# Two pairs of heads at the start of a hand-written order: scores ahead of w2's transposes, w2's fourth part ahead of v

## The chip, the cores and the metric

The kernel runs on one core of one Trainium2 chip. The metric is the device time of one execution in microseconds. The kernel before was run three times; the median counts. Beside these runs there is one execution taken by the hardware profiler, from which all durations come.

## The reference

Attention with a soft cap for 8 batches, 12 heads, 448 positions and head size 64, followed by a layer with two weights and a maximum:

```python
scores = cap * np.tanh(scale * (q @ k.T) / cap)          # cap 30
attn = np.exp(scores - max) / (sum + 1e-9)
x = (attn @ v)  -> (8 * 448, 12 * 64)
out = np.maximum(x @ w1, x @ w2) @ w_out                 # (768, 1024) twice, (1024, 768)
```

Inputs and output are float32. The kernel computes in bfloat16 with float32 sums. It doesn't subtract the row's maximum, since tanh bounds the scores. It writes the maximum as max(h1, h2) = h2 + relu(h1 - h2). So it needs x @ (w1 - w2), through a relu, times w_out, plus x @ (w2 @ w_out). The differences w1 - w2 (`wd_sb`) and the product w2 @ w_out (`wm_sb`) are made inside the kernel, in its first 60 us, beside the first pairs of heads.

## The kernel before, in words

The work is cut into **items** (two heads of one batch, 48 in all), **pairs** of items t (four heads, 24 in all) and, for the layer behind the attention, **groups** of matmuls (8 for each batch in stage 1, 6 or 8 in stage 2). No loop and no scheduler orders it. A string, `ORDER` (lines 9 to 202), lists steps by hand, and the last lines of the kernel (742 to 745) call them one after the other; each engine gets its instructions in that order, and waits for the other engines' results by semaphores. So the place of a step in the string is its place in the queue of each engine that it uses. The steps that matter here, with their lines:

- `ld0`, `cd` (L303, L308, L310): load k and q of items 0 and 1 as float32 over the SP and ACT queues, and cast them on ACT or DVE.
- `lk i`, `lq i` (L321 up to item 9, L328 after), `lv t part` (L352), `lw2 c` (L366), `lwo half part` (L360), `lw1 c` (L393): loads that cast on the way, all issued by POOL. Each of k and q is 112 KB as written, one part of w2 256 KB (512 KB as read), of w_out 384 KB, of v 128 KB. POOL has eight semaphores for its loads, so the ninth load waits until the first has landed, and so on.
- `dm`, `ms0`, `ms`, `id` (L734, L735, L289 to L292, L277): constants. `dm` sets the tile that the fillers read, `ms` the tiles of ones, `ms0` clears `ident` on DVE, and `id` writes its diagonal on POOL.
- `D bank n` (L471): idle matmuls of n units of 128 columns, four units in one instruction, whose result nobody reads. They keep PE busy where nothing else is ready.
- `X i bank` (`Xh` for half), `XC i` (L458, L463): transposes of k and q of an item on PE (28 small ones) into a PSUM bank, and DVE's copy out of it.
- `S i j`, `T i j` (L514, L519): scores of a block of 128 keys for both heads of an item (two matmuls), and their tanh on ACT. `L t`, `TL t` (L528, L532): the left-over 64 keys of a whole pair. `E i j0 j1`, `EL t` (L536, L539): the exponentials, in place.
- The scores have **two** PSUM buffers, given out in turn to S, L and VL. A step that takes a buffer waits until the tanh of its last user, or DVE's reading of the finished values, is done.
- `W c bank`, `WC c` (L416, L420): eight transposes of w2's part c on PE, and DVE's copy of them. `OP`, `P c half n`, `PC c half` (L431, L437): n matmuls of w2 @ w_out, eight for each c and half, and DVE's copy into `wm_sb`. `sub c` (L402): w1 - w2 on DVE.
- `Y t` (L566, L570, L573), `Y1` to `Y3` (L578 to L584): the sums of the exponentials, and their inverse on DVE. `VL t`, `V t u j0 j1` (L600, L606): the product with v. `N t u` (L618, L621): the division on DVE, which writes x.
- `A`, `B` (L548, L553): from pair 3 on, DVE adds the exponentials up ahead of `Y`.
- `O`, `M`, `ev`, `H`, `Hs` (L645, L640, L666, L700, L702): groups of the layer behind: open a PSUM bank, matmuls, relu or copy out. `st` (L676, L681) stores. `cr` (L475): transposes of k and q by DMA, from item 10 on.
- The other matmul results share four PSUM banks, `mm0` to `mm3`. The bank is the last number of `X`, `W`, `OP`, `Y` and `O` and the first of `D`. Who opens a bank waits until the bank's last result has been copied out.

In the first string PE gets W 2 (w2's third part) between the scores S 0 2 and S 1 0. A wait of a PE instruction holds up all that stands behind it in the string for PE.

Of the kernel before, what the change touches and what calls it, by code (L numbers as in the profile page):

```python
# [24 lines left out]
VL 2; V 2 0 0 3; V 2 1 0 3; S 7 0; OP 5 0 2; P 5 0 1; P 5 1 1; P 5 0 7; sub 0 0; Y1 2; Y2 2; Y3 2; N 2 0; N 2 1;  # L25
PC 5 1; A 3 0 1; PC 5 0; T 7 0; EL 3; lw1 1; lk 9 0; lq 10 0; lk 11 0; lw1 3; lq 9 0; lk 11 1; lv 3 1; lq 11 0;
lv 4 0; lv 3 0; lk 10 0; lw1 5; lk 10 1; O 0 0; M 0 -1 1; S 7 2; S 7 1; O 1 3; M 1 -1 1; M 0 -1 3; M 1 -1 1;
M 0 -1 2; T 7 1; T 7 2; Hs 0; S 8 0; M 1 -1 1; M 1 0 3; S 8 1; X 9 2; OP 4 1 1; P 4 1 4; sub 1 0; sub 3 0; XC 9;
E 7 0 2; T 8 1; T 8 0; P 4 1 4; L 4; O 2 2; M 2 0 2; S 8 2; M 2 0 1; M 2 1 3; A 3 0 2; A 3 1 1; B 3 1; PC 4 1;
ev 0; B 3 0; Hs 2; TL 4; E 7 2 3; T 8 2; S 9 0; O 3 1; M 3 1 3; M 3 2 3; O 4 0; M 4 2 3; VL 3; T 9 0; E 8 0 3;  # L30
A 3 1 2; ev 1; ev 2; sub 5 0; Hs 3; cr 5; V 3 0 0 1; Y 3 3; V 3 0 1 3; V 3 1 0 3; M 4 3 1; S 9 1; M 4 3 2; O 5 2;
M 5 3 3; lk 12 1; lk 13 0; lv 5 3; lq 13 0; lv 6 2; lv 4 1; lv 5 1; lk 12 0; lq 12 0; lk 15 0; lq 15 0; lk 13 1;
lq 14 0; lk 14 0; Hs 4; M 5 4 3; T 9 1; Y1 3; Y2 3; Y3 3; ev 3; N 3 1; N 3 0; Hs 5; O 6 3; M 6 4 3; M 6 5 3;
O 7 1; M 7 5 3; S 10 0; Hs 6; ev 5; A 4 0 1; ev 4; M 7 6 3; S 9 2; Hs 7; cr 6; EL 4; E 9 0 2; T 10 0; T 9 2;
O 8 2; M 8 6 2; S 10 2; M 8 6 1; M 8 7 3; S 10 1; O 9 0; M 9 7 2; T 10 2; T 10 1; E 9 2 3; M 9 7 1; VL 4;
V 4 1 0 2; L 5; TL 5; E 10 0 3; A 4 1 1; A 4 0 2; H 8; B 4 1; B 4 0; ev 7; A 4 1 2; ev 6; M 9 8 7; V 4 0 0 1;
Y 4 1; V 4 1 2 3; V 4 0 1 3; M 9 8 3; S 11 0; M 9 8 1; O 10 3; M 10 8 3; T 11 0; EL 5; Hs 9; Hs 8 2; Y1 4; Y2 4;
# [741 lines left out]
```

## Time and profile before

| what | us |
|---|---|
| three runs: median (lowest, highest) | 329.46 (329.17, 329.52) |
| the profiled execution: its own time | 329.59 |
| its span in the trace | 327.8 |
| PE busy (matmuls) | 320.3 |
| ACT busy | 281.2 |
| DVE busy | 240.2 |
| POOL busy | 161.7 |

The span runs from the first to the last instruction of the trace. Times in the trace count from its start. Matmul ends are modelled, so a PE that waits less than about 0.2 us can look busy; the step from one start to the next tells more than the length of one. The PE clock that the throttle granted was 1.0 throughout. Of DMAs the trace has the issue and the landing. In the groups and the timeline, a line stands for every step that comes through it.

### The profile page before, as it was taken

What the parts mean: (1) busy time and instruction counts of PE and PEld (TensorE: products, weight loads), DVE (VectorE), ACT (ScalarE), POOL (GpSimd) and SP (SyncE); (2) the same over time, 40 slices, a digit from 0 to 9 for tenths busy, and PEclk for the clock granted to TensorE, in tenths of its full rate; (3) what the DMA queues carried; (4) which work ended last, traced back from release to release, by engine and by line L of the source; (5) the groups of instructions that cost most, each with busy time, mean ns of one, the idle gap of its engine ahead of it and who ended that gap; (6) DMA issues with size and microseconds to landing.
All of it is one profiled execution on the core that took longest, in us unless ns stands there. A gap on an engine that the chain in (4) does not pass through costs nothing.

```text
span 327.8 us, 9768 instructions
## 1 busy us (share of the span) xinstructions
PE 320.3 (98%) x4137; PEld 184.6 (56%) x4140; DVE 240.2 (73%) x422; ACT 281.2 (86%) x278; POOL 161.7 (49%) x237
## 2 busy tenths in 40 slices
PE   8899999999999999999999999999999999999994
PEld 3445545446656664555565565556466556557662
DVE  3337889997887778987897688868878879873201
ACT  5899999999999999999999999999999999921120
POOL 8337387558862763754774675468538211000000
PEclk9999999999999999999999999999999999999999
DMA  8999999999999999999999999999999953013033
GB/s 186 193 201 134 289 185 168 115 127 137 202 187 102 118 193 194 123 79 170 165 184 90 212 138 184 109 177 142 188 114 90 211 154 46 2 50 98 0 98 96
DMA packets 134507, 46.28 MB, mean 141 GB/s; under 512 B 112320, under 2 KB 129472, under 8 KB 134464
## 3 DMA queue, kind: packets, MB, share of 16 engines
q0 software_dynamic: 94592, 25.02, 78.8%
q1 hardware_dynamic: 39424, 19.99, 28.2%
q8 instruction: 32, 0.52, 0.7%
q10 hardware_dynamic: 448, 0.66, 0.5%
q14 instruction: 11, 0.09, 0.1%
HBM read 47.78 MB, written 11.01 MB: 179 GB/s over the span
## 4 chain that ended last, share of the span: by engine, by line
PE 86%; DVE 6%; DMA 6%; POOL 1%; issue 1%; POOLq 0%; DVEq 0%
PE mm L645 58%; PE s L514 8%; PE s L606 8%; DMA w2b<-in_moe_w_dram 3%; PE mm L431 3%; DMA osb<-in_moe_w_dram 2%; PE s L528 2%; PE mm L573 1%; PE mm L640 1%; PE s L600 1%; DVE wd_sb L402 1%; PE mm L416 1%; DVE gT L666 1%; DVE xT L621 1%; POOL kqs L321 1%; PE mm L458 1%
## 5 line engine op out<-in xcount | busy, mean ns | idle before, releaser
L519 ACT ACTIVATE e<-s 128x896 bf16<-128x896 f32 x144 | 125.8, 928 | 6.3 <-PE s L514 6.0
L536 ACT ACTIVATE e<-e 128x1792 bf16<-128x1792 bf16 (+2 forms) x72 | 123.2, 1712 | 0.0
L645 PE MATMUL mm<-wo_sb,gT 64*128 64x384 bf16 x864 | 115.5, 323 | 0.0
L645 PE MATMUL mm<-wm_sb,xT 64*128 64x384 bf16 x648 | 101.9, 323 | 0.1
L645 PE MATMUL mm<-xT,wd_sb 64*128 64x448 bf16 x768 | 97.2, 350 | 0.0
L328 POOL DMA_DIRECT2D kqs<-in_k_dram x76 | 54.7, 721 | 54.0 <-DMA qkT<-kqs 49.9
L645 PEld LDWEIGHTS <-gT 64*128 64x128 bf16 x864 | 58.7, 94 | 25.4 <-issue 1.1
L645 PEld LDWEIGHTS <-wd_sb 64*128 64x128 bf16 x768 | 48.9, 94 | 27.2 <-issue 2.4
L645 PEld LDWEIGHTS <-xT 64*128 64x128 bf16 x648 | 50.5, 94 | 18.3 <-issue 0.2
L514 PE MATMUL s<-qkT 64*128 64x448 bf16 x288 | 51.8, 352 | 0.0
L352 POOL DMA_DIRECT2D vp<-in_v_dram x48 | 30.6, 642 | 34.3 <-PE s L514 26.4
L666 DVE TENSOR_SCALAR gT<-mm 128x448 bf16<-128x448 f32 x64 | 38.9, 617 | 8.6 <-PE mm L645 7.6
L328 POOL DMA_DIRECT2D kqs<-in_q_dram x38 | 35.1, 925 | 5.9 <-PE mm L458 5.0
L606 PE MATMUL s<-e,vp 128*32 128x448 bf16 x576 | 36.0, 354 | 0.0
L548 DVE TENSOR_TENSOR esum<-e 128x896 bf16<-128x896 bf16 x42 | 26.0, 618 | 9.9 <-ACT e L536 9.9
L621 DVE TENSOR_TENSOR xT<-s,inv 64x448 bf16<-64x448 f32 x48 | 29.9, 622 | 0.9
L548 DVE TENSOR_TENSOR esum<-esum,e 128x896 bf16<-128x896 bf16 x42 | 26.2, 623 | 5.8 <-ACT e L536 4.8
L514 PEld LDWEIGHTS <-qkT 64*128 64x128 bf16 x288 | 18.4, 94 | 19.2 <-issue 11.0
L700 ACT COPY osb<-mm 128x384 f32<-128x384 f32 x10 | 4.8, 478 | 26.9 <-PE mm L645 26.7
L702 DVE COPY osb<-mm 128x384 f32<-128x384 f32 x44 | 23.3, 554 | 5.0 <-PE mm L645 4.5
L553 DVE TENSOR_TENSOR esum<-esum,el 64x896 bf16<-64x896 bf16 x42 | 26.0, 619 | 1.2
L578 DVE STREAM_TRANSPOSE st<-mm 128x448 f32<-128x448 f32 x24 | 15.6, 649 | 13.2 <-PE mm L573 11.6
(57 smaller groups left out, 269.8 us busy)
## 6 DMA issues: line engine op xcount, KB each, us to landing
out_dram<-osb SPq DMA_DIRECT2D x54, 192.0 KB, 4.3
vp<-in_v_dram POOLq DMA_DIRECT2D x38, 160.0 KB, 4.0
kqs<-in_q_dram POOLq DMA_DIRECT2D x46, 112.0 KB, 5.6
kqs<-in_k_dram POOLq DMA_DIRECT2D x76, 56.0 KB, 3.9
osb<-in_moe_w_dram POOLq DMA_DIRECT2D x4, 512.0 KB, 8.6
w2b<-in_moe_w_dram POOLq DMA_DIRECT2D x6, 256.0 KB, 6.8
wo_sb<-in_moe_w_out_dram POOLq DMA_DIRECT2D x4, 384.0 KB, 8.3
vp<-in_v_dram POOLq DMA_DIRECT2D x10, 128.0 KB, 6.8
```

Source lines behind the costliest of these rows:

```text
L328: nc.gpsimd.dma_start(out=to, in_=x)
L352: nc.gpsimd.dma_start(out=to, in_=x)
L514: scored[i, j] = nc.tensor.matmul(s[:, h, :S], k_of(t, o, h, j), q_of(t, o, h)).ins
L519: nc.scalar.activation(expo[i][:, 2 * j : 2 * j + 2, :], slots[i, j][:, :, :S], AF.Tanh, scale=scale / cap)
L536: nc.scalar.activation(e, e, AF.Exp, scale=float(cap))
L548: nc.vector.tensor_add(d, e[:, 0:2, :] if j == 1 else d, e[:, 2 * j : 2 * j + 2, :])
L553: nc.vector.tensor_add(d, d, left_e[t][r, :, :])
L606: nc.tensor.matmul(vals[t][place(m, u), u, :S], w[:, m, :], expo[2 * t + o][:, 2 * j + h, :], start=False, stop=(j == NJ - 1))
L621: nc.vector.tensor_mul(x[64 - r : 128 - r], vals[t][r : r + 64, u, :S], sums[t, 3][64 - r : 128 - r])
L645: ins = nc.tensor.matmul(self.ps, w[r], x[r], start=first, stop=self.at == [self.n, self.n]).ins
L666: nc.vector.tensor_relu(gT[b // 2][:, f, cs], ps)
L702: nc.vector.tensor_copy(o[:, hs], ps)
```

## The change

Only the string changes, and only its first part: up to its 434th step of 2328 (the 438th of 2332 after it), which before runs at some 75 us. From there on both strings hold the same steps in the same order, and only the numbers of the four shared banks are given out anew. In the first part nearly the same steps are there in another order, some cut into more or fewer pieces:

- POOL: `id` comes ahead of all loads. Then q2, k3, q3, k2 (before k3, k2, q3, q2). w2's parts come as 3, 2, 1 (before 2, 3, 1). w2's part 0 (the fourth to be loaded), q4 and k4 come ahead of both parts of the first pair's v; the second half of w_out follows at once, then q5, k5 and the second pair's v.
- DVE: the tiles of ones are set ahead of the fillers' tile and `ident`.
- PE: S 0 2, L 0, S 1 2, S 1 0, X 3 and X 2 now all stand ahead of the first W (W 3, then W 2). X 4 comes ahead of VL 0, Y 0, V 0; X 5 after S 4 0 and S 3 2. W 5 comes after S 6 0 and S 6 1. The premultiplications are dealt out anew between these.
- ACT: T 1 0 comes behind the exponential of item 0.
- D: 24 units instead of 32 ahead of the first transposes, 72 units behind them as before, in more pieces.

```diff
-ld0 k; ld0 k 1; ld0 q; ld0 q 1; dm; ms0; lk 3 0; lk 2 0; lq 3 0; id; D 3 8; ms; cd q; cd k; lq 2 0; lw2 2; lw2 3;
-lw2 1; D 3 24; Xh 0 0 0; Xh 0 1; cd k 1 1; cd q 1 1; XCh 0 1; XCh 0 0; D 3 5; X 1 1; S 0 1; S 0 0; XC 1; T 0 1;
-T 0 0; D 0 5; D 1 12; L 0; D 1 8; S 0 2; W 2 0; TL 0; T 0 2; S 1 0; X 3 2; D 1 26; X 2 1; S 1 2; T 1 0; E 0 0 3;
-T 1 2; lwo 0 0; lwo 0 1; lv 0 1; lw2 0; lv 0 0; lk 5 0; lq 5 0; lq 4 0; lk 4 0; lwo 1 0; lv 1 1; lwo 1 1; WC 2;
-XC 3; XC 2; S 1 1; W 3 3; W 1 2; D 0 16; S 2 1; WC 1; WC 3; T 1 1; E 1 2 3; T 2 1; S 2 0; OP 1 0 1; P 1 0 1;
-OP 3 0 3; P 3 0 3; OP 2 0 0; P 2 0 3; P 1 0 1; P 2 0 1; P 1 0 2; L 1; P 3 0 1; P 1 0 2; P 3 0 1; P 2 0 1; P 1 0 1;
-P 3 0 1; P 2 0 3; P 3 0 2; PC 3 0; PC 2 0; T 2 0; E 1 0 2; TL 1; EL 0; S 2 2; S 3 0; Y 0 2; P 1 0 1; W 0 0; T 2 2;
-T 3 0; VL 0; V 0 0 0 3; V 0 1 0 3; S 3 1; X 4 3; lv 1 0; lk 8 0; lw2 5; lq 6 0; lk 7 0; lk 6 0; lw2 4; lq 8 0;
-lw1 4; lq 7 0; lw1 2; lw1 0; lv 2 1; lv 2 0; WC 0; Y1 0; Y2 0; PC 1 0; Y3 0; XC 4; N 0 0; N 0 1; E 2 0 3; T 3 1;
-EL 1; E 3 0 2; X 5 0; OP 0 0 2; P 0 0 5; OP 1 1 3; P 1 1 4; P 0 0 1; OP 2 1 1; P 2 1 3; S 4 0; S 3 2; P 0 0 1;
-P 2 1 2; P 0 0 1; P 1 1 3; P 2 1 3; P 1 1 1; XC 5; PC 0 0; PC 2 1; PC 1 1; T 3 2; T 4 0; E 3 2 3; OP 3 1 2;
-P 3 1 2; S 4 1; S 4 2; Y 1 1; T 4 1; T 4 2; L 2; P 3 1 4; VL 1; V 1 0 0 3; V 1 1 0 3; TL 2; E 4 0 3; S 5 0;
-P 3 1 2; W 4 3; T 5 0; EL 2; Y1 1; Y2 1; Y3 1; N 1 0; N 1 1; WC 4; PC 3 1; X 6 1; X 8 0; S 5 1; S 5 2; W 5 2;
-XC 8; XC 6; sub 4 0; WC 5; T 5 1; T 5 2; OP 4 0 0; P 4 0 8; S 6 0; X 7 1; OP 0 1 3; P 0 1 8; S 6 1; E 5 0 2;
-T 6 0; E 5 2 3; T 6 1; PC 4 0; XC 7; sub 2 0; PC 0 1; S 6 2; OP 5 1 1; P 5 1 7; L 3; T 6 2; TL 3; E 6 0 3; Y 2 3;
...
+ld0 q; ld0 q 1; cd q; ld0 k; ld0 k 1; ms; dm; ms0; cd k; id; lq 2 0; lk 3 0; lq 3 0; lk 2 0; lw2 3; lw2 2; D 3 24;
+Xh 0 0 0; Xh 0 1; cd k 1 1; cd q 1 1; XCh 0 1; XCh 0 0; D 3 4; X 1 1; S 0 0; S 0 1; XC 1; T 0 0; T 0 1; D 0 5;
+D 1 8; D 3 1; D 1 4; S 0 2; D 1 4; L 0; D 1 16; T 0 2; TL 0; E 0 0 3; D 1 12; S 1 2; S 1 0; X 3 3; X 2 0; W 3 2;
+W 2 1; T 1 0; T 1 2; lw2 1; lwo 0 0; lwo 0 1; lw2 0; lq 4 0; lk 4 0; lv 0 0; lv 0 1; XC 3; XC 2; WC 3; D 0 4;
+S 1 1; D 0 8; D 2 2; S 2 1; W 1 2; WC 2; WC 1; T 1 1; T 2 1; S 2 0; D 0 4; L 1; OP 3 0 0; P 3 0 2; OP 1 0 1;
+P 1 0 4; P 3 0 2; OP 2 0 3; P 2 0 7; P 1 0 1; P 2 0 1; P 1 0 1; P 3 0 2; P 1 0 2; PC 2 0; PC 1 0; E 1 2 3;
+E 1 0 2; TL 1; T 2 0; EL 0; S 3 0; S 2 2; P 3 0 1; W 0 2; P 3 0 1; X 4 3; T 2 2; T 3 0; VL 0; Y 0 1; V 0 0 0 3;
+V 0 1 0 3; S 3 1; lwo 1 0; lwo 1 1; lq 5 0; lk 5 0; lv 1 0; lv 1 1; lk 8 0; lq 8 0; lq 7 0; lw2 4; lv 6 2; lq 6 0;
+lk 7 0; lk 6 0; lw2 5; lw1 2; lw1 4; lw1 0; lv 2 0; lv 2 1; WC 0; PC 3 0; XC 4; Y1 0; Y2 0; Y3 0; N 0 0; N 0 1;
+E 2 0 3; T 3 1; EL 1; E 3 0 2; OP 0 0 1; P 0 0 2; OP 2 1 2; P 2 1 2; P 0 0 1; OP 1 1 3; P 1 1 2; P 0 0 1; P 1 1 2;
+P 0 0 1; P 1 1 4; S 4 0; S 3 2; X 5 0; P 2 1 4; P 0 0 3; P 2 1 1; XC 5; PC 1 1; PC 0 0; T 3 2; T 4 0; E 3 2 3;
+OP 3 1 3; P 3 1 1; P 2 1 1; S 4 1; S 4 2; Y 1 1; T 4 1; T 4 2; L 2; P 3 1 4; VL 1; TL 2; V 1 1 0 3; V 1 0 0 3;
+S 5 0; X 6 0; E 4 0 3; T 5 0; EL 2; Y1 1; Y2 1; PC 2 1; Y3 1; N 1 1; N 1 0; XC 6; X 7 2; W 4 1; S 5 2; S 5 1;
+X 8 0; P 3 1 3; WC 4; XC 8; PC 3 1; T 5 1; T 5 2; OP 4 0 1; P 4 0 2; OP 0 1 0; P 0 1 3; S 6 0; S 6 1; W 5 3;
+P 0 1 1; P 4 0 6; P 0 1 4; E 5 0 2; T 6 1; T 6 0; E 5 2 3; XC 7; sub 2 0; WC 5; sub 4 0; PC 4 0; sub 0 0; PC 0 1;
+OP 5 1 3; P 5 1 4; S 6 2; L 3; Y 2 1; T 6 2; TL 3; E 6 0 3; VL 2; V 2 1 0 1; V 2 0 0 3; V 2 1 1 3; S 7 0; P 5 1 4;
...
```

More of the change, by code (lines that the diff above doesn't have):

```diff
@@ L25 @@
[L25 to L29, printed above, removed]
@@ new lines @@
+M 9 8 7; S 11 0; M 9 8 1; O 10 3; M 10 8 3; E 10 0 3; T 11 0; EL 5; Hs 9; Hs 8 2; Y1 4; M 10 9 3; Y2 4; Y3 4;
+N 4 1; N 4 0; M 8 9 2; S 11 1; M 8 9 3; S 11 2; M 8 9 3; lv 5 2; lk 15 0; lk 14 0; lv 6 1; lk 14 1; lq 14 0;
+lv 5 1; lq 16 0; lv 6 3; lv 6 0; lk 16 1; lk 17 0; lk 16 0; T 11 1; T 11 2; E 11 0 2; O 11 0; M 11 9 3; S 12 0;
+M 11 10 6; S 12 1; M 11 10 1; ev 8; ev 9; A 5 0 1; A 5 0 2; lk 17 1; M 11 10 4; T 12 0; lq 17 0; O 12 1;
+M 12 10 1; A 5 1 1; M 12 10 1; Hs 11; cr 7; M 12 10 1; M 12 11 1; B 5 0; M 12 11 1; T 12 1; M 12 11 1; S 12 2;
@@ new lines @@
+H 10 2; B 5 1; M 10 11 1; T 12 2; M 10 11 5; E 11 2 3; st 0 0; M 10 11 2; O 13 2; M 13 11 1; ev 10; L 6; VL 5;
+A 5 1 2; TL 6; V 5 0 0 2; V 5 1 0 2; Y 5 3; E 12 0 3; V 5 0 2 3; V 5 1 2 3; Y1 5; S 13 0; M 13 11 1; lv 7 0;
+M 13 11 1; Y2 5; M 13 12 2; Y3 5; M 13 12 1; lv 7 1; M 13 12 3; N 5 0; M 13 12 1; lv 7 2; M 13 12 1; T 13 0;
+M 13 12 1; N 5 1; M 13 12 1; lv 7 3; M 13 12 1; O 14 3; M 14 12 2; EL 6; Hs 13; S 13 1; lk 18 0; M 14 12 1;
+M 14 13 1; ev 11; M 14 13 1; Hs 12 2; T 13 1; S 13 2; lk 18 1; M 14 13 1; A 6 0 1; M 12 13 2; T 13 2; Hs 14;
@@ new lines @@
+M 23 21 1; Hs 22; lq 21 0; M 23 21 1; M 23 22 2; ev 21; M 23 22 1; T 16 0; M 23 22 2; A 7 1 1; M 23 22 2; cr 9;
+M 23 22 1; T 16 1; M 23 22 1; B 7 0; S 16 2; M 23 22 2; B 7 1; O 24 1; M 24 22 1; T 16 2; M 24 22 2; H 23;
+M 24 23 1; H 22 2; E 15 2 3; M 24 23 2; M 22 23 1; L 8; VL 7; A 7 1 2; TL 8; V 7 0 0 2; V 7 1 0 2; Y 7 2;
+E 16 0 3; V 7 0 2 3; lk 22 0; V 7 1 2 3; Y1 7; S 17 0; M 22 23 1; lv 9 0; M 22 23 1; Y2 7; M 22 23 2; Y3 7;
+M 22 23 1; lv 9 1; M 22 23 2; O 25 2; M 25 23 1; N 7 0; M 25 23 1; lv 9 2; M 25 23 1; T 17 0; M 25 24 1; N 7 1;
@@ new lines @@
+E 17 2 3; M 27 26 1; O 28 1; M 28 26 2; L 9; VL 8; A 8 1 2; TL 9; V 8 0 0 2; V 8 1 0 2; Y 8 2; E 18 0 3;
+V 8 0 2 3; V 8 1 2 3; Y1 8; lk 24 0; st 1 4; S 19 0; M 28 26 1; M 28 27 1; Y2 8; M 28 27 1; Hs 26 2; lv 10 0;
+M 28 27 1; Y3 8; M 26 27 3; Hs 28; lv 10 1; M 26 27 1; N 8 0; M 26 27 2; T 19 0; M 26 27 1; lv 10 2; N 8 1;
+M 26 27 1; O 29 2; M 29 27 3; EL 9; lv 10 3; M 29 28 1; S 19 1; M 29 28 2; lk 24 1; ev 26; M 29 28 1; T 19 1;
+S 19 2; M 29 28 1; ev 27; M 29 28 1; lq 24 0; M 29 28 1; T 19 2; M 29 28 1; A 9 0 1; S 20 0; M 29 28 2; A 9 0 2;
@@ new lines @@
+ev 104; M 106 105 1; O 107 2; M 107 105 2; Hs 106; M 107 105 1; M 107 106 2; ev 105; M 107 106 1; O 108 3;
+M 108 106 2; Hs 107; M 108 106 1; M 108 107 2; ev 106; st 6 2; M 108 107 1; O 109 0; M 109 107 2; H 108;
+M 109 107 1; M 109 108 2; ev 107; M 109 108 1; O 110 1; M 110 108 2; Hs 109; M 110 108 1; M 110 109 2; ev 108;
+M 110 109 1; O 111 2; M 111 109 2; Hs 110; M 111 109 1; M 111 110 2; ev 109; M 111 110 1; O 112 3; M 112 110 2;
+Hs 111; M 112 110 1; M 112 111 2; ev 110; M 112 111 1; O 113 0; M 113 111 2; Hs 112; M 113 111 1; M 113 112 2;
```

235 lines of the change are left out of this document (107 added, 128 removed).

## The prediction

> **What bounds the kernel now.** I read the windows first, to see which engine has no slack, then PE's waits, then PE, ScalarE (ACT), VectorE (DVE) and GpSimd (POOL) along the first 40 us, where the change lies. The windows:
>
> ```profile
> 80.00:295.00 215.00, 215.00 (x2816) 126.23 (x2810) 177.41 (x312) 203.08 (x197) 111.73 (x158) 1.00 1.17 140
> ```
>
> From 80 to 295 us PE (third number) is busy for all of 215.00 us and ACT for 203.08 (sixth). From there on the two orders hold the same steps. So PE bounds the kernel, and a microsecond that PE loses or saves ahead of that part comes out at the end, as long as ACT, with 12 us of slack there, doesn't fall behind. The change is worth what PE waits, or fills with idle matmuls, at the start. PE along the start (start, length, line, count, and in brackets its idle time before):
>
> ```profile
> 1.19 3.59 PE L471 MATMUL mm<-warm 128*128 128x512 bf16 x8 [1.19 <-DVE warm L734]
> 4.72 0.63 PE L458 MATMUL mm<-ident,kqs 64*64 64x64 bf16 x28
> 5.28 0.45 PE L471 MATMUL mm<-warm 128*128 128x512 bf16 x2
> ...
> 6.50 0.55 PE L514 MATMUL s<-qkT 64*128 64x448 bf16 x4
> 6.99 1.11 PE L471 MATMUL mm<-warm 128*128 128x512 bf16 x4
> 8.03 0.38 PE L528 MATMUL s<-qkT 64*32 64x448 bf16 x8
> 8.34 0.60 PE L471 MATMUL mm<-warm 128*128 128x512 bf16 x2
> 8.88 0.36 PE L514 MATMUL s<-qkT 64*128 64x448 bf16 x2
> 10.40 0.62 PE L416 MATMUL mm<-ident,w2b 128*128 128x128 bf16 x8 [1.15 <-DMA w2b<-in_moe_w_dram]
> 10.95 0.36 PE L514 MATMUL s<-qkT 64*128 64x448 bf16 x2
> 11.24 0.63 PE L458 MATMUL mm<-ident,kqs 64*64 64x64 bf16 x28
> 12.03 1.35 PE L471 MATMUL mm<-warm 128*128 128x512 bf16 x6 [0.16 <-issue]
> ...
> 16.83 1.96 PE L431 MATMUL mm<-wo_sb,w2T 128*128 128x384 bf16 x11
> 18.72 0.38 PE L528 MATMUL s<-qkT 64*32 64x448 bf16 x8
> ...
> 21.58 0.75 PE L566 MATMUL mm<-e,ones 128*32 128x448 bf16 x12
> ...
> 24.73 0.36 PE L514 MATMUL s<-qkT 64*128 64x448 bf16 x2
> ...
> 38.28 0.61 PE L416 MATMUL mm<-ident,w2b 128*128 128x128 bf16 x8 [0.53 <-DMA osb<-in_moe_w_dram]
> ```
>
> The reader is to see three things. At 10.40 PE has waited 1.15 us for w2's first part (step W 2 0), with the second item's scores (S 1 0, 10.95) queued behind it. At 12.03 it loses 0.16, at 38.28 another 0.53. And from one start to the next the rows give what each step takes of PE: four score matmuls 0.49, two 0.29, a left-over step L 0.31, eight transposes of w2 0.55, 28 of k and q 0.56 (4.72 to 5.28), one premultiplication 0.172 (11 from 16.83 to 18.72). A filler of 512 columns takes about 0.22 (six in 1.35), as does each further 4 units of D. ACT at the same time:
>
> ```profile
> 6.91 1.73 ACT L519 ACTIVATE e<-s 128x896 bf16<-128x896 f32 x2 [0.80 <-PE s L514]
> 8.52 0.93 ACT L532 ACTIVATE el<-s 128x896 bf16<-128x896 f32 x1
> 9.31 0.94 ACT L519 ACTIVATE e<-s 128x896 bf16<-128x896 f32 x1
> 11.36 0.92 ACT L519 ACTIVATE e<-s 128x896 bf16<-128x896 f32 x1 [1.10 <-PE s L514]
> 12.17 2.44 ACT L536 ACTIVATE e<-e 128x2688 bf16<-128x2688 bf16 x1
> ```
>
> ACT loses 1.10 us at the same place: S 1 0 stands behind the wait for w2. A tanh takes 0.92 and starts each 0.80; the exponential of a whole item takes 2.33 to the next start; a tanh starts 0.43 after its two score matmuls (8.88 to 9.31). The scores have two PSUM buffers, so each S or L waits for a tanh: L 0 started at 8.03, 0.20 after the first tanh ended (6.91 + 0.92), S 0 2 at 8.88, 0.24 after the second (8.64).
>
> **The change, part by part.** *Fillers.* In units of 128 columns, D has 32 ahead of the first transposes before and 24 after; behind them 72 in both. The eight lie ahead of 4.72, where the transposes wait for the cast of k in any case:
>
> ```profile
> 4.08 0.56 DVE L310 CAST kqs<-kr 128x448 bf16<-128x448 f32 x1 [2.37 <-DMA kr<-in_k_dram]
> ```
>
> It ends at 4.64. So the eight are worth nothing, and the 72 only change places.
>
> *Scores ahead of W 2 and W 3.* I step through PE's new order with those durations, from S 0 0 at 6.50 (its inputs come over the ACT and SP queues, whose order is the same).
> - 0.49 of scores, 18 units of fillers (0.98): 7.97. S 0 2 waits for its buffer to 8.03, ends 8.32. Four units: 8.54. L 0 waits for the second tanh to 8.88 (0.34 lost), ends 9.19. 28 units (1.52): 10.71. S 1 2 and S 1 0: 11.20. X 3, X 2 (1.12): 12.32. W 3, W 2 (1.10): 13.42.
> - ACT has the left-over tanh at 9.40 and the exponential at 10.19, so T 1 0 at 12.53 and T 1 2 at 13.33. What ACT had done at 14.50 before (12.17 + 2.33) it has done at 13.33: 1.17 earlier.
> - Four units: 13.64. S 1 1 needs T 1 0's end (13.45 + 0.20): no wait; 13.93. Ten units: 14.47. S 2 1, W 1, S 2 0: 15.60. Four units: 15.82. L 1 waits for T 2 1 (14.93 + 0.92 + 0.22) to 16.07: 0.25 lost; 16.38. 22 P (3.78), S 3 0 and S 2 2, P, W 0, P, X 4: 22.10.
> - Then VL 0, Y 0 and V 0. The row at 21.58 stands for Y 0, and to 24.73 it is followed by one P, W 0, VL 0 and V 0: 3.15, less 0.72 for P and W, is 2.43. S 3 1 is at 24.53. Before it is at 24.73, but without X 4 (0.56), which is 25.29 at equal work. **Gain here: 0.76.** Waits of 1.15 + 0.16 + 0.22 (two short ones, at 8.03 and 8.88) have gone; 0.06 + 0.34 + 0.25 have come; the rest is rounding.
>
> *The wait at 38.28.* The page puts it down to a DMA, but W 5 opens a PSUM bank, and DVE empties that bank just then:
>
> ```profile
> 37.68 0.55 DVE L437 CAST wm_sb<-mm 128x384 bf16<-128x384 f32 x1
> ```
>
> It ends at 38.23, 0.05 ahead of W 5: that is what PE waits for, and DVE comes late because it copied w2's fourth transposed part first. In the new order X 8, three P, two P, three P and the scores S 6 0, S 6 1 stand ahead of W 5, some 2.5 us of PE: the 0.53 goes. What is late next are the tanhs and DVE: S 4 2, Y 1 and L 2 now ask ACT sooner than it has gained, and Y 4 asks DVE for the last sum. I take 0.45 in all for them, an estimate from the three waits worked out above (0.06, 0.34, 0.25); bounds are 0 and, if each of these four loses 0.34, 1.36.
>
> *The load queue.* POOL issues the loads, at most eight in flight: the ninth waits for the first. Now `id` stands ahead of all of them and needs the memset of `ident`, which DVE does after `ones`.
>
> ```profile
> 1.24 1.24 POOL L321 DMA_DIRECT2D kqs<-in_k_dram  x2 [0.79 <-POOLq L760]
> ...
> 3.07 0.33 POOL L277 TENSOR_SCALAR_AFFINE_SELECT ident<-ident 128x128 bf16<-128x128 bf16 x1
> ...
> 3.85 1.62 POOL L366 DMA_DIRECT2D w2b<-in_moe_w_dram  x3
> ```
>
> The first load goes out at about 2.05 instead of 1.24 (estimate: memset done near 1.7, then 0.33), and `id` no longer stands between loads, so w2's first part is issued near 4.4 instead of 3.85. The landing of that first w2 part, from a window with its issue alone, and of the last part of the first pair's v (when issued, then to landing):
>
> ```profile
> DMA to landing us min/median/max: 6.5/6.5/6.5
> ```
>
> ```profile
> L352 POOL DMA_DIRECT2D vp<-in_v_dram x1: 717/717/717, 8.0 to 8.0; - x1
> ...
> DMA to landing us min/median/max: 11.8/11.8/11.8
> ```
>
> ```profile
> 11.00:25.00 14.00, 13.73 (x186) 7.22 (x187) 5.95 (x11) 13.64 (x13) 4.81 (x8) 1.00 1.29 200
> ```
>
> The first part landed at 10.35, v at 19.8. The queue is full up to 25 us, at 200 GB/s (last number of the window, bytes as written), so landings go by bytes ahead in the queue: w2's second part, 256 KB more, at about 11.6. New, the first w2 part lands between 10.35 and 10.9 and W 3 asks at 12.32; the second between 11.6 and 12.2, asked for at 12.87. v has q and k of item 4 ahead of it as well, 224 KB, 1.1 us: 20.9 to 21.5, and VL 0 asks at 22.10. All in time, with 0.6 us to spare at worst. Loads further back land no later in sum, as the same bytes are ahead of them.
>
> The Trainium skill speaks against the change here: "DMA: Bandwidth & Descriptors", section "Anatomy of one DMA — SWDGE (gpsimd) path", gives about 2.0 us plus bytes over 436 GB/s for a DMA. For 512 KB that is 3.2 us (estimate from the page), so w2 would be there at 7.1, PE would not have waited for it, and moving the scores forward would bring nothing. The row says 6.5, behind other loads; the row decides.
>
> **Sum.** 0.76 + 0.53 − 0.45 = 0.84 us less. The profiled execution took 329.59 us (its span and 1.8 us around it), 0.13 over the median of the runs, 329.46. From the median: **328.6 us**.
>
> **Rivals.**
> 1. *All that goes stays gone.* No wait for tanhs or DVE comes later, and L 0 and L 1 wait less: 1.15 + 0.16 + 0.53 less 0.34 is 1.50: 327.9. For it: ACT is 1.17 ahead too. Against: two score buffers tie PE to ACT.
> 2. *ACT and DVE take it back.* ACT has nothing but tanhs and exponentials in a row from 12 us on; a PE that comes sooner waits for it. With the 1.36 for later waits the sum is 0.76 + 0.53 − 1.36, about nothing: 329.5.
> 3. *The load stream comes later (the other side).* Behind `id`, the whole queue may slip by more than the 0.55 that I take. The spare is 0.6 at VL 0, 0.7 at W 2; each microsecond beyond holds PE for a microsecond in steps with nothing to pass them. Slower than before it is from 1.5 us of further lateness (0.6 spare and 0.84 gain); at 2.2 us: 328.6 + 1.6 = 330.2. For it: v is moved behind 224 KB more, and the first part took 6.5 us. Against: the queue is full up to 25 us, so a late start is made good while the first k and q load.
> 4. *A cold clock.* PE's first fillers step by 0.43 (eight from 1.19 to 4.72), later ones by 0.22; the 28 transposes at 4.72 are fast. New, fillers start about 0.47 later, end near 4.2, and PE pauses to 4.7. If PE then stays slow for another 3.5 us, to 8.2, the transposes, scores and fillers in it take twice as long, part of it under waits for casts and tanhs: about 0.8 lost, 329.4. Against: PE has run for 2.5 of the 3.5 us. The Trainium skill, "TensorE: Matmul & The Clock Gate", section "Part 1: The HAM clock gate", has the clock double after about 3.4 us of activity in a free-running window, which the 3.5 us here agree with; no run here shows a window that is partly idle.
>
> **How the numbers follow.** My forecast has 0.50, its own range is 328.1 to 329.2; rival 1 0.11, rival 2 0.12, rival 3 0.22, rival 4 0.05. A measurement of this kernel can tell about 0.2%, 0.66 us: faster is below 328.80, slower above 330.12. Faster: 0.33 of the forecast and rival 1, 0.44. Same: 0.17 of the forecast, rivals 2 and 4 and 0.03 of rival 3, 0.37. Slower: the rest of rival 3, 0.19. The range takes in rival 1 and rival 3 at 2.2 us, 327.8 to 330.3, and leaves out a still later stream.
>
> **What would show it.** Right: PE's wait for w2b ahead of 12 us gone; ACT without a gap between 9 and 14 us; S 3 1 (L514, two matmuls ahead of 11 or more of L431) near 24.5; X 4's transposes ahead of it; no PE wait near 38; PE busy from 80 to the end as before, everything about 0.8 earlier. Wrong: PE waits for `vp` or `w2b` in the first 25 us (rival 3), fillers or transposes after 4.7 at double length (rival 4), PE gaps at L528 or L573 that add up to more than 1 us (rival 2). The first w2 landing after 12.3, or v's after 22.1, would undo the forecast.

## The result, and the profile after

| kernel | median, us (lowest to highest, runs) | against the kernel before | 95% interval |
|---|---|---|---|
| before | 329.38 (329.17 to 329.52, 9) | | |
| after | 328.48 (327.89 to 328.74, 9) | 0.9971 | 0.9963 to 0.9979 |
| after, measured again | 328.35 (327.93 to 329.34, 9) | 0.9974 | 0.9962 to 0.9985 |

The change is worth 0.9 to 1.1 us, 0.3% (the second measurement ran on another chip, on which the kernel before took 329.44); the forecast was 328.6. The profiled execution took 328.69, its span is 326.9 (327.8 before). From 80 to 295 us, TensorE (PE), in the third column, is busy without a break again:

```profile
80.00:295.00 215.00, 215.00 (x2807) 126.20 (x2805) 176.99 (x311) 202.25 (x196) 112.02 (x158) 1.00 1.19 140
```

The last long group of matmuls starts at 318.12 (319.03 before) and the scores S 11 0 at 69.62 (70.56): all of the difference is made in the first 70 us. PE's waits in the kernel after (us in total, times, longest):

```profile
PE mm L471 <- DVE warm L734: 1.8, 1, 1.8
PE mm L416 <- DMA w2b<-in_moe_w_dram: 0.5, 1, 0.5
PE s L514 <- DVE xT L618: 0.2, 1, 0.2
```

The 1.2 us for w2's first landing and the 0.5 at 38.28 are gone. There is a new wait for w2, of 0.5 us. PE's timeline shows whose it is:

```profile
1.79 2.74 PE L471 MATMUL mm<-warm 128*128 128x512 bf16 x6 [1.79 <-DVE warm L734]
...
6.42 0.55 PE L514 MATMUL s<-qkT 64*128 64x448 bf16 x4
...
8.62 0.38 PE L528 MATMUL s<-qkT 64*32 64x448 bf16 x8
...
10.55 0.55 PE L514 MATMUL s<-qkT 64*128 64x448 bf16 x4
...
12.04 1.19 PE L416 MATMUL mm<-ident,w2b 128*128 128x128 bf16 x16
...
15.20 0.62 PE L416 MATMUL mm<-ident,w2b 128*128 128x128 bf16 x8 [0.52 <-DMA w2b<-in_moe_w_dram]
...
16.37 0.38 PE L528 MATMUL s<-qkT 64*32 64x448 bf16 x8
...
22.36 0.48 PE L600 MATMUL s<-el,vp 64*32 64x448 bf16 x8
...
24.78 0.36 PE L514 MATMUL s<-qkT 64*128 64x448 bf16 x2
...
36.55 0.55 PE L514 MATMUL s<-qkT 64*128 64x448 bf16 x4 [0.16 <-DVE xT L618]
37.08 0.63 PE L458 MATMUL mm<-ident,kqs 64*64 64x64 bf16 x28
37.64 1.47 PE L431 MATMUL mm<-wo_sb,w2T 128*128 128x384 bf16 x8
39.05 0.55 PE L514 MATMUL s<-qkT 64*128 64x448 bf16 x4
39.53 0.62 PE L416 MATMUL mm<-ident,w2b 128*128 128x128 bf16 x8
```

The reader is to see: W 3 and W 2 run at 12.04 without a wait that the page names (they take 1.02 to the next start and 0.91 in a later trace, so W 2 lost 0.1 at most); W 1, which takes the part of w2 that is issued third, waits 0.52 at 15.20; S 3 1 is at 24.78; W 5 is at 39.53, without a wait. ScalarE (ACT) has no gap from 9 to 20 us and starts the first pair's exponentials at 10.03, and waits for PE only at 21.04:

```profile
10.03 2.46 ACT L536 ACTIVATE e<-e 128x2688 bf16<-128x2688 bf16 x1
12.36 3.37 ACT L519 ACTIVATE e<-s 128x896 bf16<-128x896 f32 x4
...
21.04 1.73 ACT L519 ACTIVATE e<-s 128x896 bf16<-128x896 f32 x2 [0.44 <-PE s L514]
```

The loads on GpSimd (POOL) start where the forecast had them, the first at 2.12 and w2 from 4.56:

```profile
1.88 0.29 POOL L277 TENSOR_SCALAR_AFFINE_SELECT ident<-ident 128x128 bf16<-128x128 bf16 x1 [1.43 <-DVE ident L735]
2.12 0.69 POOL L321 DMA_DIRECT2D kqs<-in_q_dram  x1
...
4.56 1.61 POOL L366 DMA_DIRECT2D w2b<-in_moe_w_dram  x3
```

They land later than it had them. A view of w2's second and third parts alone (issued at 5.1 and 5.6) gives the times from issue to landing:

```profile
L366 POOL DMA_DIRECT2D w2b<-in_moe_w_dram x2: 558/562/566, 5.1 to 5.6; - x2
...
DMA to landing us min/median/max: 7.5/8.5/9.6
```

5.1 and 7.5 make 12.6 for the second part, 0.4 later than the forecast's latest. 5.6 and 9.6 make 15.2 for the third, which is when W 1 starts. The last part of v took 9.6 from 12.8 and landed at 22.4; VL 0 asks at 22.36.

### The profile page after: what moved, and what is told of

It reads as the page before. It is cut to its first block, busy times and chain, and to the rows that moved or that the text cites. A ratio compares the mean times of both kernels' runs of the same rounds, so it can differ in the third digit from the quotient of the medians.

```text
span 326.9 us, 9772 instructions
## 1 busy us (share of the span) xinstructions
PE 320.2 (98%) x4138; PEld 184.5 (56%) x4138; DVE 240.1 (73%) x422; ACT 281.1 (86%) x278; POOL 162.2 (50%) x237
## 4 chain that ended last, share of the span: by engine, by line
PE 93%; DMA 3%; POOL 1%; DVE 1%; issue 0%
PE mm L645 61%; PE s L514 9%; PE s L606 9%; PE mm L431 5%; DMA w2b<-in_moe_w_dram 3%; PE s L528 2%; PE s L600 2%; PE mm L573 2%; PE mm L640 1%; POOL kqs L321 1%; PE mm L458 1%; PE mm L566 1%; PE mm L416 0%; DVE xT L621 0%; POOL w2b L366 0%; DVE xT L618 0%
## 5 line engine op out<-in xcount | busy, mean ns | idle before, releaser
L514 PE MATMUL s<-qkT 64*128 64x448 bf16 x288 | 52.7, 352 | 0.2 <-DVE xT L618 0.2
```

Of the source, the lines that this page charges most:

```text
L514: scored[i, j] = nc.tensor.matmul(s[:, h, :S], k_of(t, o, h, j), q_of(t, o, h)).ins
```

## The experiments

The times are medians of 5 to 12 runs each; the ratio is against the kernel before, run on the same chip (329.36 to 329.44 there). "Trace" stands for one profiled execution of the kernel.

| run | median, us (lowest to highest) | ratio, 95% interval |
|---|---|---|
| before with PC 3 1 first | 329.30 (329.01 to 329.85) | 1.0001, 0.9993 to 1.0010 |
| before with PC 3 1 first and two banks exchanged | 328.93 (328.50 to 329.27) | 0.9983, 0.9974 to 0.9992 |
| before with S 1 0 ahead of W 2 | 329.02 (328.88 to 329.14) | 0.9988, 0.9980 to 0.9997 |
| the same with less filler | 328.47 (328.32 to 329.03) | 0.9978, 0.9969 to 0.9986 |
| before with less filler alone | 329.32 (328.90 to 329.45) | 0.9995, 0.9986 to 1.0004 |
| after without 28 units of filler | 328.80 (328.42 to 330.52) | 0.9987, 0.9975 to 1.0000 |
| after with late `id` and DVE's order changed | 329.40 (327.97 to 330.71) | 1.0000, 0.9984 to 1.0015 |
| the same with eight fillers at the start | 328.00 (327.86 to 328.41) | 0.9957, 0.9945 to 0.9970 |
| after with late `id` alone | 328.02 (327.94 to 329.37) | 0.9956, 0.9942 to 0.9969 |
| after with v ahead of w2's last part | 328.81 (328.43 to 329.82) | 0.9984, 0.9976 to 0.9993 |
| before with both gains | 327.83 (327.69 to 328.44) | 0.9954, 0.9941 to 0.9966 |

**The wait at 38.28.** The theory was that W 5 waits for its bank, which VectorE (DVE) empties late; the rival was the page's own label, a DMA.

```diff
-N 1 0; N 1 1; WC 4; PC 3 1; X 6 1;
+N 1 0; N 1 1; PC 3 1; WC 4; X 6 1;
```

> The kernel before, with one step moved: the copies of PC 3 1 ahead of the four of WC 4 on VectorE. Nothing else is changed, the loads least of all. My theory: W 5 waits 0.53 us at 38.28 because the bank that it writes is emptied by PC 3 1's last copy, which ended at 38.23. With PC 3 1 done 0.6 us earlier the wait is 0.1 us or less, nothing in the stage behind takes it back, and the time is 0.4 to 0.5 us below the kernel before: 328.9 to 329.0. Rival, the page's own reading: the wait is for a transfer of w2; it stays at 0.5 us and the time is that of before, within 0.1 us. Second rival: the four copies of WC 4, now later, hold up XC 8 and the scores behind it, and the 0.5 us come back as a wait before 50 us: 329.4.

Measured: no change. PE's timeline of this run:

```profile
37.54 0.61 PE L416 MATMUL mm<-ident,w2b 128*128 128x128 bf16 x8
38.67 1.46 PE L431 MATMUL mm<-wo_sb,w2T 128*128 128x384 bf16 x8 [0.52 <-DVE qkT L463]
```

and DVE's:

```profile
36.92 0.56 DVE L437 CAST wm_sb<-mm 128x384 bf16<-128x384 f32 x1
37.40 0.68 DVE L420 COPY w2T<-mm 128x1024 bf16<-128x1024 bf16 x1
38.00 1.15 DVE L463 COPY qkT<-mm 128x896 bf16<-128x896 bf16 x2
```

W 5 starts at 37.54, right behind the scores and without a wait; PC 3 1's copy had ended at 37.48 (36.92 + 0.56). Only that copy was moved and no DMA was touched, so the wait was for the copy. (In two other variants, which leave this part of the order as it was, the page itself puts the same 0.54 down to DVE's copy, `wm_sb` L437.) But the same 0.52 stands one step further on. P 4 0 opens bank 0, and bank 0 is emptied by the first of the two copies that start at 38.00 (about 0.58 each). The label "DVE qkT" is right this time. So the time had the second rival's result, and the forecast of 0.5 for this move alone was wrong. What was left to tell apart: is DVE as a whole too late here, or only the bank that P 4 0 got?

```diff
-N 1 0; N 1 1; WC 4; PC 3 1; X 6 1;
+N 1 0; N 1 1; PC 3 1; WC 4; X 6 1;
...
-OP 4 0 0; P 4 0 8; S 6 0; X 7 1; OP 0 1 3; P 0 1 8;
+OP 4 0 3; P 4 0 8; S 6 0; X 7 1; OP 0 1 0; P 0 1 8;
```

> The kernel before with PC 3 1 ahead of WC 4, and with the banks of two later sums exchanged: P 4 0 in bank 3 (emptied by WC 4) and P 0 1 in bank 0 (emptied by the first copy of XC 8). With PC 3 1 moved alone W 5's wait went, and a wait of 0.52 us came at P 4 0, which writes bank 0. My theory now: TensorE has nothing without a bank there, VectorE empties the banks one after the other (N 1, PC 3 1, WC 4, XC 8), and P 4 0 waits because its bank is the last one to be emptied, not because its data are late. With bank 3 it starts at about 38.1, the wait of 0.5 us is gone, and the time is 328.8 to 328.9. Rival: it is VectorE as a whole that is late there, so the wait comes up a third time, at S 6 0, X 7 or P 0 1, and the time is that of before, 329.3.

```profile
37.49 0.62 PE L416 MATMUL mm<-ident,w2b 128*128 128x128 bf16 x8
38.09 1.47 PE L431 MATMUL mm<-wo_sb,w2T 128*128 128x384 bf16 x8
39.49 0.36 PE L514 MATMUL s<-qkT 64*128 64x448 bf16 x2
```

Measured 328.93, 0.5 below before, and PE's timeline runs through. The bank it is, not DVE as a whole. The changed kernel does the same by its own means: its P 4 0 opens bank 1, and W 5 has moved behind two scores.

**Scores ahead of w2.** Theory: PE sets the end, so of the 1.2 us of waiting only the work moved into it is gained, the rest only where fillers go too. Rival: ACT sets the end, and its 1.1 us of lead come out in full.

```diff
-S 0 2; W 2 0; TL 0; T 0 2; S 1 0; X 3 2; D 1 26;
+S 0 2; TL 0; T 0 2; S 1 0; W 2 0; X 3 2; D 1 26;
```

> The kernel before, with W 2 put behind TL 0, T 0 2 and S 1 0, so that TensorE does S 1 0 (0.29 us) while w2's second part is still on its way, and ScalarE gets that score earlier. The 26 units of filler stay. My theory (TensorE sets the end): of the 1.2 us of waiting in that stretch only the work moved into it is gained, so 0.3 us: 329.1, with the wait for w2 down by about 0.3 us. Rival (ScalarE's chain of tanh and exp sets the end of the stage): its exp of pair 1 begins about 1.1 us earlier and the whole of that comes out at the end: 328.3.

Measured 329.02. ACT starts its first exponentials at 10.74 in the trace (12.17 before), 1.4 us earlier, and the kernel gains 0.3 to 0.4. The rival that ACT sets the end is out. PE's timeline of this run:

```profile
9.32 0.36 PE L514 MATMUL s<-qkT 64*128 64x448 bf16 x2 [0.25 <-ACT el L532]
10.12 0.62 PE L416 MATMUL mm<-ident,w2b 128*128 128x128 bf16 x8 [0.43 <-DMA w2b<-in_moe_w_dram]
```

In this trace w2's first part also landed 0.28 earlier than in the one before (W 2 at 10.12 against 10.40), with the same loads, so the gain is read from the medians and not from the trace.

Then the same with `D 1 10` in place of `D 1 26`, and, as its counterpart, `D 1 10` alone in the kernel before. The cut takes out four instructions of up to 512 columns, on dead data.

> As the run above, with 16 of the 26 units of filler behind X 3 2 left out as well (16 multiplications on dead data, 0.86 us of TensorE); no output depends on them. My theory: with the scores of pair 1 ahead of w2, ScalarE hands over its tanh 1.1 us earlier, so the filler is no longer cover for a wait but work on the path, and the run gains about 0.3 from the score moved and 0.8 from the filler: 328.3, about where the changed kernel is. Rival (TensorE waits for the tanh in any case): the 0.86 us come back as waits at S 2 1 and S 2 0 and the time is that of the run above.

> The kernel before with only the filler behind X 3 2 cut from seven instructions to three (0.86 us of TensorE), and the scores left behind w2. With the scores moved as well the cut was worth 0.5 us. My theory: with the scores of pair 1 behind w2, ScalarE's tanhs come as late as in the kernel before, S 2 1 and S 2 0 wait for the score buffers that these free, and the filler is cover: 329.3, at most 0.15 us below the kernel before. Rival (TensorE alone is the bound in this stretch): 0.5 to 0.8 us below it, 328.6 to 328.9.

Measured 328.47 and 329.32. The same cut is worth 0.55 us behind the moved scores and nothing clear of the noise (0.09) where they were not moved. There PE waits in its place, at S 2 0 (16.05) and at L 2 (32.16), as its waits in the kernel before with less filler show:

```profile
PE s L514 <- ACT e L519: 0.4, 1, 0.4
PE s L528 <- ACT e L519: 0.2, 1, 0.2
```

So ahead of the scores' move filler is cover for the tanhs; behind it, it is work on the path. Both engines have to come forward together, and the changed kernel does both.

Does the changed kernel's own filler still cost anything?

```diff
-L 0; D 1 16; T 0 2; TL 0; E 0 0 3; D 1 12;
+L 0; T 0 2; TL 0; E 0 0 3;
```

> The changed kernel without its seven instructions of filler around E 0 0 3 (1.5 us of TensorE between 8.9 and 10.9 us); no output depends on them. My theory: they are cover. TensorE comes 1.5 us earlier to the transposes and to w2's first parts, waits there until 11.4 us for the landing, then for the tanhs of pair 1, which run without a gap on ScalarE from 9 to 14 us, and for w2's third part: no gain, 328.3 to 328.6. Rival (TensorE alone is the bound): up to 0.9 us less, 327.6. Rival on the other side: without filler the clock falls back and the transposes and turns up to 16 us run at half speed: 329 or more.

```profile
6.79 0.92 PE L514 MATMUL s<-qkT 64*128 64x448 bf16 x4
...
8.72 0.36 PE L514 MATMUL s<-qkT 64*128 64x448 bf16 x2
...
10.10 0.37 PE L514 MATMUL s<-qkT 64*128 64x448 bf16 x2 [0.37 <-ACT e L519]
10.91 0.37 PE L514 MATMUL s<-qkT 64*128 64x448 bf16 x2 [0.44 <-ACT el L532]
11.20 1.07 PE L458 MATMUL mm<-ident,kqs 64*64 64x64 bf16 x56
...
14.04 0.36 PE L514 MATMUL s<-qkT 64*128 64x448 bf16 x2 [0.55 <-ACT e L519]
```

In place of 1.5 us of filler PE waits 0.37 + 0.44 + 0.55 = 1.36 us for tanhs. From S 0 2 (8.72) to S 1 1 (14.04) it takes 5.32 us, with the filler 5.37 (8.00 to 13.37): cover. ACT's rows show the tanhs that it waits for first:

```profile
7.39 2.65 ACT L519 ACTIVATE e<-s 128x896 bf16<-128x896 f32 x3 [1.17 <-PE s L514]
9.94 0.91 ACT L532 ACTIVATE el<-s 128x896 bf16<-128x896 f32 x1
```

They end at 10.04 and 10.85, and PE starts 0.06 after each. The transposes at 11.20 take what they take in the kernel after (1.07 for 56), so the clock did not fall back. The median, 328.80, is 0.2 over what I expected. The profiled execution, 328.72, lost its time ahead of the cut: its first four scores ran slowly (6.79 to 7.64) and S 0 2 came 0.72 later than in the kernel after. Whether that is what raised the median is not shown.

**The load stream.** Theory: `id` ahead of the loads starts them 0.9 us late, and this is why W 1 waits. Rival: the order of the loads is to blame.

```diff
-ms; dm; ms0; cd k; id; lq 2 0; lk 3 0; lq 3 0; lk 2 0;
+dm; ms0; lq 2 0; lk 3 0; lq 3 0; id; ms; cd k; lk 2 0;
```

> The changed kernel, with the identity, the filler's memset and one more step put behind the first three loads of q and k on GpSimd, so that the first load is issued at about 1.2 us, as in the kernel before, and not at 2.1; the order of the loads stays. My theory: the stream of loads of the changed kernel runs about 1 us late because it starts late, which is why W 1 waits 0.52 us for w2's third part at 15.2 and why v lands at 22.4. With the start taken back W 1 waits 0.1 us or less, v lands at about 21.5, and the time is 0.3 to 0.5 us below the changed kernel: 328.0 to 328.2. Rival: the order of the loads (w2's fourth part and its copies behind the other parts) makes the stream slow between 6.5 and 14.5 us; then w2's third part still lands at 15, W 1 still waits 0.4 to 0.5 us and the time is that of the changed kernel. What could take it back: the filler's data comes later, so TensorE's first filler starts later and the scores at 6.4 run at a lower clock.

Measured 329.40, between 327.97 and 330.71: not the gain I expected. W 1 no longer waits (PE has no wait for w2 in this trace). The time is lost ahead of it, as PE's timeline shows:

```profile
1.19 2.74 PE L471 MATMUL mm<-warm 128*128 128x512 bf16 x6 [1.19 <-DVE warm L734]
4.69 0.96 PE L458 MATMUL mm<-ident,kqs 64*64 64x64 bf16 x28 [0.75 <-DVE kqs L310]
...
7.00 0.93 PE L514 MATMUL s<-qkT 64*128 64x448 bf16 x4
```

I had moved `dm` ahead of `ms` as well, so the six fillers began at 1.19 and not at 1.79, and PE stood still for 0.75 us until the cast of k. What follows runs slowly: 28 transposes and four scores start their successors 0.89 and 0.86 later, where 0.56 and 0.48 are usual. Two runs take this apart: one fills the pause (`D 3 32` for `D 3 24`), one moves `id` alone.

```diff
-ms; dm; ms0; cd k; id; lq 2 0; lk 3 0; lq 3 0; lk 2 0;
+ms; dm; ms0; cd k; lq 2 0; lk 3 0; lq 3 0; id; lk 2 0;
```

> The changed kernel with the loads started at 1.2 us as in the run with the late identity, and with eight instructions of filler ahead of the first transposes, not six (D 3 32 for D 3 24). In that run TensorE stood still for 0.75 us ahead of the first transposes, ran at half speed up to about 7.9 us, and the times spread from 328.0 to 330.7. My theory: the pause was the cause, a half-idle stretch that puts off the faster clock; the load stream itself was cured. With the pause filled the transposes and scores up to 7 us run fast, W 1 waits 0.1 us or less for w2's third part, v lands by 21, and the time is 328.0 (327.8 to 328.2), with a spread under 1 us. Rival: the clock is slow by chance of the run, whatever fills the pause; then the spread stays over 2 us and the median near 329.4. Second rival: the load stream's start is worth nothing, 328.5.

> The changed kernel with one step moved on GpSimd: the identity behind the first three loads of q and k instead of ahead of them. VectorE's order and the six instructions of filler from 1.8 us on stay as in the changed kernel. The run that also began the filler at 1.2 us, with eight instructions, took 328.0. My theory: of its 0.5 us against the changed kernel most is the load stream, which now starts 0.5 to 0.8 us sooner; W 1's wait of 0.52 us for w2's third part is gone or under 0.1, S 3 1 starts near 24.3 (24.78 in the changed kernel), and the time is 328.1 to 328.2. Rival: the gain was the earlier filler (a faster clock at the first transposes in more of the runs); then the time is that of the changed kernel, 328.4 to 328.7, although the wait is gone from the trace.

Measured 328.00 and 328.02: both 0.3 to 0.5 below the kernel after by the medians, and alike, so the earlier filler adds nothing. PE's timeline with `id` alone moved has no wait at W 1, and S 3 1 comes 0.72 earlier than in the kernel after:

```profile
14.63 0.62 PE L416 MATMUL mm<-ident,w2b 128*128 128x128 bf16 x8
...
24.06 0.36 PE L514 MATMUL s<-qkT 64*128 64x448 bf16 x2
```

The intervals of the ratios just overlap with those of the kernel after (up to 0.9970 and from 0.9962), so the gain is not clear of the noise. The profiled execution with `id` alone moved was its slowest by far, 329.37 against four of 327.94 to 328.03; in it the scores at 96.84 waited 1.20 us for a transpose by DMA, a wait that the other traces don't have. A late transfer further on can thus cost more than what is argued about here. What the loads moved from 6.5 to 14.5 us stands in the last column, GB/s; first the kernel after, then the one with `id` alone moved:

```profile
6.50:14.50 8.00, 8.00 (x112) 3.84 (x112) 2.97 (x5) 7.68 (x8) 4.03 (x7) 1.00 1.08 157
```

```profile
6.50:14.50 8.00, 7.97 (x114) 3.98 (x112) 2.98 (x5) 7.63 (x8) 4.18 (x7) 1.00 1.18 184
```

157 against 184 over 8 us is 0.22 MB, more than 1 us of loads at 200 GB/s. That is more than the 0.7 us by which the w2 loads were issued later (4.56 against 3.83), and why is open. The landings say the same: with `id` behind the loads w2's third part, issued at 4.9 to 5.1, was there at 12.3 to 12.9 in three traces; with `id` ahead, issued at 5.6 in this one, at 15.2. Traces with `id` ahead of the loads show 150 to 173, those with it behind 184 to 191, the kernel before 182; the order of the loads behind is the same in both, so the rival on the order falls.

Two variants with the late start had w2's third part in time all the same (13.9 and 14.2). So I took the changed kernel again.

> The changed kernel once more, for a second profile and more times. In its first profile the loads moved 157 GB/s from 6.5 to 14.5 us, w2's third part landed at 15.2 and W 1 waited 0.52 us; two variants with the same start of the loads moved 172 and 150 and had that part there at 13.9 and 14.2, ahead of W 1. My theory: with the late start w2's third part comes close to the time at which W 1 asks for it (14.7 us), so some executions wait and some do not: a profiled execution without the wait takes 328.0 to 328.3, one with it 328.5 or more, and the times spread over 0.6 to 1.0 us around 328.4. Rival: the wait is there each time; then the second profile shows it too, at 0.4 us or more, and the two shortest of the nine times so far, 327.89 and 327.96, have another reason.

This time the profiled execution took 328.19, and PE's timeline has no wait at W 1:

```profile
6.68 0.55 PE L514 MATMUL s<-qkT 64*128 64x448 bf16 x4
...
14.85 0.62 PE L416 MATMUL mm<-ident,w2b 128*128 128x128 bf16 x8
...
24.27 0.36 PE L514 MATMUL s<-qkT 64*128 64x448 bf16 x2
```

The part landed at 14.7 (5.4 + 9.3), just ahead of W 1. So the wait is there in some executions and not in others, from 0 to 0.52 us by two profiles. The nine times spread from 327.93 to 329.34, more than this wait accounts for. From the first scores to S 3 1 this trace takes 17.59 us (6.68 to 24.27) and the one with `id` alone moved 17.60 (6.46 to 24.06): where W 1 doesn't wait anyway, the early load stream gained nothing up to there.

**v behind w2's last part.** The change puts v behind w2's fourth part and q and k of item 4, and the forecast found room for it.

```diff
-lw2 0; lq 4 0; lk 4 0; lv 0 0; lv 0 1;
+lv 0 0; lv 0 1; lw2 0; lq 4 0; lk 4 0;
```

> The changed kernel with its two loads of v issued ahead of w2's fourth part and of q and k of item 4. My theory: landings go by the bytes ahead in the queue. v then lands about 2 us sooner, near 20.2, and w2's fourth part and k of item 4 land 1 us later or more, at about 21 and 22; W 0 (at 20.9) and X 4 (at 21.8) then wait 0.2 to 0.7 us together, and the time is 0.2 to 0.6 us above the changed kernel: 328.7 to 329.1. Rival: in the changed kernel v is what TensorE waits for at 22.4, and with v first the time is up to 0.1 us below it: 328.4.

Measured 328.81. PE's waits in this run:

```profile
PE mm L458 <- DMA kqs<-in_k_dram: 0.3, 1, 0.3
PE mm L416 <- DMA w2b<-in_moe_w_dram: 0.3, 1, 0.3
```

X 4 waits 0.30 for k of item 4, as expected, W 0 not at all, and w2's second part, which I had not named, is 0.26 late at 12.97. The move can't be the reason for that, as the loads ahead of this part are the same; it is the spread of a landing. S 3 1 starts at 24.75, where the first trace of the kernel after, with its wait at W 1, has it. Against that trace v lands at 19.5 and not at 22.4, w2's fourth part at 20.7 and not at 19.9, k of item 4 at 21.9 and not at 21.0. So the order in the queue decides who waits; that the order of the change is better by 0.3 to 0.5 us rests on the medians alone, and the intervals of the ratios overlap.

**A version that beats both.** The kernel before with S 1 0 ahead of W 2, `D 1 10`, PC 3 1 first and the two banks exchanged:

> The kernel before with the two independent gains together: S 1 0 ahead of W 2 with four instructions of filler fewer (0.9 us by itself), and PC 3 1 first with the two banks exchanged (0.5 us by itself). The first is at the start of the kernel, the second at 38 us. My theory: TensorE sets the end in both places and nothing between or behind gives it back, so they add: 329.4 less 1.4 is 328.0, under the changed kernel's 328.5. Rival: what comes earlier at 38 us waits there for something else (VectorE, which has 1.9 us of normalising just ahead): 328.4.

Measured 327.83, 1.6 us below before and 0.5 to 0.65 below after (five runs; the interval of the ratio meets that of the kernel after at its edge, 0.9966 and 0.9962). The two gains add: 0.89 and 0.48 by themselves. Its profiled execution, 328.44, was again the slowest of the five, with a slow start: its first scores are at 7.08.

## Why the prediction was right, and where it was not

The forecast was 0.84 us less than before, the result 0.90 and 1.09. The sum was nearly right, its terms less so; that they came out so near is in part luck.

- *PE bounds the kernel, a microsecond at the start comes out at the end.* Right. S 11 0 is 0.94 earlier in the first trace and 1.44 in the second, the spans 0.9 and 1.4 shorter. ACT's lead of 1.4 us alone gave 0.3 to 0.4.
- *Scores ahead of W 2 and W 3, 0.76 at S 3 1.* Right in kind, mis-sized. Against 25.29 the traces of the changed kernel have 24.78 and 24.27, so 0.51 and 1.02, and with the loads started early 24.06, so 1.23. The steps that failed are the waits for score buffers, 0.34 at L 0 and 0.25 at L 1. L 0 came at 8.62, not 8.88, 0.08 after the second tanh ended (6.82 + 0.80 + 0.92). L 1 came at 16.04 in the second trace, 0.05 after T 2 1's tanh ended (12.62 + 3.37), with about 0.1 lost. The hand-over of 0.20 to 0.24 that I had read from L 0 and S 0 2 in the kernel before was no hand-over: fillers stood ahead of both, and where PE did wait for a tanh, without the 28 units, it was 0.06. Some durations were too long as well: X 3, X 2, W 3 and W 2 in a row took 1.91 (11.29 to 13.20 in the second trace), not 2.22.
- *Loads: in time, with 0.6 us to spare at worst.* Wrong. The starts were right (2.12 and 4.56 against 2.05 and 4.4). But "the queue is full up to 25 us", from which I took that a late start is made good, did not hold: from 6.5 to 14.5 us the loads moved 157 GB/s where the kernel before has 182. v landed at 22.4, not by 21.5, and cost VL 0 at most 0.1. And I worked out landings for w2's first and second parts and for v, but none for the third, which is where PE waited. By the same working (1.3 us for 256 KB at 200 GB/s) it would have been there by 13.5, in time; so what failed is the rate, and not only the landing that I left out. The sign that the prediction gives for rival 3, a wait for `w2b` in the first 25 us, did come, at 0.52.
- *The wait at 38.28, 0.53.* It goes, and it was DVE's copy, not the DMA that the page names. But "DVE comes late because it copied w2's fourth part first" was not the whole cause: with the copies exchanged the wait moved one step on. P 4 0's bank had to come free too.
- *Later waits, 0.45.* Too much. From S 3 1 to S 11 0 the changed kernel gains another 0.43 (0.94 less 0.51) and 0.42 (1.44 less 1.02), so 0.1 of the 0.53 was taken back; 0.16 at S 5 2 is the only such wait that PE's list has.

So errors in opposite directions, too much taken for buffer waits and later waits and too little for the loads, left the sum near. Rival 1, 327.9, is where the fastest times of the changed kernel lie (327.89 and 327.93), but not its medians. Rival 2 is out: ACT took nothing back. Rival 3 named the right mechanism, a load stream that comes later, but for v and with PE held for far longer. By the medians the two gains alone give 1.6 us (the last experiment), and the late load stream takes 0.3 to 0.5 of that back in the changed kernel; the second figure is not clear of the noise. Rival 4's pause did not come: fillers ran from 1.79 to 4.53, and the transposes followed within 0.2. Slow steps at the start showed all the same, in several kernels, before as well as after, and are next.

## What the runs showed of the chip

*When PE gets fast differs from run to run.* With fillers from 1.19 on and no pause, 28 transposes take 0.56 to the next start at 4.72 in the kernel before, but 0.88 to 0.89 in four of its variants. In three of them the first scores then come at 6.88 to 7.08 instead of 6.50; in the fourth the next transposes are fast again and the scores come at 6.54. With fillers from 1.78 on, four scores take 0.48 to the next start in both traces of the kernel after (at 6.42 and 6.68), and 0.85 (at 6.79) in the run without the 28 units, though its order is the same up to there. All of them show a granted clock of 1.00, so that column does not show it; the steps do. The Trainium skill, "TensorE: Matmul & The Clock Gate", section "Part 1: The HAM clock gate", has the clock double after a busy window of about 3.4 us that runs free, so that the same kernel has a different number of slow matmuls in each run; these starts agree. After the pause of 0.75 us PE was slow up to 7.86. That the pause did it is supported by the run that filled it (328.41 at most in five runs). But chance alone has cost 0.72 at S 0 2 in the run without the 28 units, against 1.0 to 1.2 here (9.23, with 8.00 and 8.26 in the traces of the kernel after), so it is not proved; nor do the profiles explain the times up to 330.7 of the run with the pause.

*The landing of one and the same load differs by more than a microsecond.* Issued third of w2, at 5.4 to 5.6 us, a part of 256 KB landed at 13.9, 14.2, 14.7 and 15.2 in four traces with `id` ahead of the loads. The Trainium skill, "DMA: Bandwidth & Descriptors", section "Anatomy of one DMA — SWDGE (gpsimd) path", would give 3.2 us for its 512 KB as read (an estimate from that page); the rows have 8.3 to 9.6, in a queue with other loads ahead.

## What to carry to other kernels

- A wait for a bank or buffer is a place in the emptying engine's row: list all that the row frees there before costing a move, because the next step in line may be waiting for the copy behind.
- Filler may be cover or cost; it turns from one into the other when the engine that it waits for comes forward, so try the move with and without it.
- Where loads share one queue, work out the landing of every part that a moved step reads, and not only of the first and the last; and give a landing a range of a microsecond from run to run.
